# KV on four 64x64 tiles and two banks instead of two 128x64 tiles and one

## Chip, cores, metric

One core of one Trainium2 chip. The metric is the device time in microseconds (us) of one execution. The page and the trace of a kernel come from one profiled execution, whose span is 1.7 to 1.8 us shorter than its time (470.9 of 472.63 us before).

## The reference, cut to what matters

```python
qkv = (x @ wqkv)...                                   # x is 2048 x 1024, 32 heads of 32
kv  = jnp.einsum("bhsd,bhse->bhde", phi(k), v)        # branch A, linear attention
num = jnp.einsum("bhqd,bhde->bhqe", phi(q), kv)
a   = (num / den) @ wo
out = g * a + (1 - g) * b                             # b: a local attention over 8 positions
```

The kernel never forms v for branch A. It computes G = x^T phi(k) (1024 x 1024), then KV = Wv^T G for each pair of heads (a 64x64 block), and folds KV into the output weights ("W2").

## The kernel before

```python
# G: 16 banks, each 16 matmuls of 128x512, copied out by ScalarE            (cut)
for g in range(2):                                    # two groups of 16 heads
    kvp = ps_pj.tile([P, 512], F32, name="kv_ps", tag="pj")[:, 0:256].rearrange("p (c d) -> p c d", c=4)
    for c in range(4):
        for kt in range(KT):                          # KT = 8 blocks of 128 of the contraction
            for j in range(2):                        # two column tiles, 128 rows x 64 columns
                cols = slice(c * P + 64 * j, c * P + 64 * j + 64)
                nc.tensor.matmul(kvp[64 * j:64 * j + 64, c, :], lhsT=WvA[g][:, kt, cols],
                                 rhs=G[g][:, kt, cols], start=(kt == 0), stop=(kt == KT - 1))
    nc.vector.tensor_copy(out=KVT[:, 4 * g:4 * g + 4, :], in_=kvp)
WkB = load_w("WkB", B_wqkv, D, "wb")                  # into the buffers of WvA
...
w2_event(0, 0, ps_1, "p1", both)()                    # W2: 16 matmuls on 32x32 tiles; reads KVT of group 0
interleave(units, [(32, w2_event(0, 1, ps_1, "p1", both))])   # V projections, 128x512
```

The softmax here doesn't subtract the row's maximum and nothing guards it: scores larger than these inputs give would overflow.

## Time and profile before

| | before |
|---|---|
| time, median of the first 3 runs | 472.31 us (472.19 to 472.64) |
| profiled span, mean granted clock | 470.9 us, 1.000 |
| KV's first matmul to W2's first instruction | 116.38 to 118.53, 2.15 us |
| TensorE instructions in it | 256 (128 weight loads, 128 matmuls) |
| first V projection | 118.90 |

TensorE is the bound all along (busy for 99% of the span), so the table follows TensorE's time line. Most of the lines are in the prediction; the V projections that follow start so (start us, length us):

```profile
118.90 3.41 PE L294 MATMUL p_ps<-WvB,xT 128*128 128x512 bf16 x14
```

### The profile page before, as it was taken

To read this page: it belongs to the slowest core of one execution; us is meant where nothing else is said; L and a number is where in the kernel's file an instruction comes from. 1 tells how busy PE (TensorE), PEld (TensorE's weight loads), DVE (VectorE), ACT (ScalarE), POOL (GpSimd) and SP (SyncE) were. 2 spreads that over 40 slices of the span, in tenths; PEclk is the share of its full clock that TensorE was granted. 3 is DMA by queue.
4 is the path that set the end of the run, shared out by engine and by line. 5 is a ranking of instruction groups with operands and counts; after the bars stand their busy time and mean duration, and the time that the engine had idled before them with its cause. 6 is when DMAs were issued, how large, how long until landed. Compare 5 with 4: busy or idle time off the path is not lost.

```text
span 470.9 us, 13162 instructions
## 1 busy us (share of the span) xinstructions
PE 465.3 (99%) x5735; PEld 269.8 (57%) x5765; DVE 275.3 (58%) x598; ACT 169.1 (36%) x276; POOL 15.3 (3%) x30
## 2 busy tenths in 40 slices
PE   8999999999999999999999999999999999999997
PEld 5444444445444444444888888888874444444444
DVE  0596689990219999999666676767660049800000
ACT  1343321102433333334555555555553134221121
POOL 3300000500000000000000000000000000000000
PEclk9999999999999999999999999999999999999999
DMA  8999970000644233627325523442463923211001
GB/s 202 226 243 375 348 237 0 0 1 0 204 136 134 81 141 123 155 97 251 105 55 108 108 59 82 101 92 59 88 167 74 213 78 79 71 53 45 34 33 46
DMA packets 98732, 55.40 MB, mean 118 GB/s; under 512 B 70130, under 2 KB 90610, under 8 KB 98674
## 3 DMA queue, kind: packets, MB, share of 16 engines
q1 hardware_dynamic: 93378, 49.87, 39.9%
q10 hardware_dynamic: 5296, 4.69, 2.9%
q8 instruction: 45, 0.74, 0.6%
q14 instruction: 13, 0.11, 0.1%
HBM read 26.10 MB, written 15.86 MB: 89 GB/s over the span
## 4 chain that ended last, share of the span: by engine, by line
PE 86%; SPq 10%; DMA 2%; issue 1%; DVE 0%; DVEq 0%
PE q_ps L390 26%; PE d_ps L596 12%; PE p_ps L294 12%; PE e_ps L596 11%; PE g_ps L233 11%; PE p_ps L330 9%; SPq L115 4%; SPq L81 3%; DMA WvB<-in_B_wqkv_dram 2%; PE po L470 2%; PE s2b L448 2%; SPq L94 1%; SPq L98 1%; SPq L89 1%; SPq L119 1%
## 5 line engine op out<-in xcount | busy, mean ns | idle before, releaser
L390 PE MATMUL q_ps<-xT,WqB 64*64 64x512 bf16 x1024 | 70.3, 377 | 0.0
L390 PE MATMUL q_ps<-xT,WkB 64*64 64x512 bf16 x1024 | 69.8, 376 | 0.0
L156 DVE TENSOR_SCALAR e<-e 128x512 f32<-128x512 f32 x64 | 27.0, 423 | 68.3 <-ACT e L155 68.3
L294 PE MATMUL p_ps<-WvB,xT 128*128 128x512 bf16 x250 | 56.9, 379 | 0.3
L182 PE MATMUL pk_ps<-WkA,xT 128*128 128x512 bf16 x251 | 55.6, 381 | 0.7 <-DMA xT<-in_A_x_dram 0.4
L233 PE MATMUL g_ps<-pk,xrow 128*128 128x512 bf16 x251 | 55.2, 379 | 0.3
L453 ACT ACTIVATE PT<-s2b 128x928 bf16<-128x928 f32 (+4 forms) x40 | 34.2, 856 | 50.0 <-PE s2b L448 49.0
L455 DVE TENSOR_TENSOR PT<-PT,mask 128x928 bf16<-128x928 bf16 (+4 forms) x40 | 23.6, 590 | 36.3 <-ACT PT L453 36.3
L390 PEld LDWEIGHTS <-WkB 64*64 64x64 bf16 x1024 | 40.4, 107 | 6.9 <-DMA vd<-tmp 0.2
L330 PE MATMUL p_ps<-WqA,xT 128*128 128x512 bf16 x188 | 43.2, 379 | 0.3
L596 PEld LDWEIGHTS <-pqT 128*128 128x128 bf16 x272 | 26.0, 98 | 29.6 <-issue 0.2
L596 PEld LDWEIGHTS <-OBT 128*128 128x128 bf16 x272 | 26.0, 98 | 29.4
L182 PEld LDWEIGHTS <-xT 128*128 128x128 bf16 x256 | 25.1, 98 | 31.0 <-DMA xT<-in_A_x_dram 0.7
L390 PEld LDWEIGHTS <-WqB 64*64 64x64 bf16 x1024 | 39.4, 107 | 5.6 <-DVE qz L430 0.2
L233 PEld LDWEIGHTS <-xrow 128*128 128x128 bf16 x256 | 25.0, 98 | 30.2
L294 PEld LDWEIGHTS <-xT 128*128 128x128 bf16 x256 | 24.9, 98 | 30.2 <-issue 0.5
L603 DVE TENSOR_SCALAR osb<-e_ps,omg 128x128 bf16<-128x128 f32 x1 | 0.4, 351 | 57.6 <-PE e_ps L596 57.6
L155 ACT ACTIVATE e<-pk_ps 128x512 f32<-128x512 f32 x32 | 18.9, 597 | 40.6 <-PE pk_ps L182 36.4
L470 PEld LDWEIGHTS <-PT 64*56 64x56 bf16 (+2 forms) x1152 | 29.9, 104 | 4.5
L299 ACT CAST tmp<-p_ps 128x512 bf16<-128x512 f32 x32 | 18.7, 589 | 37.0 <-PE p_ps L294 26.6
L330 PEld LDWEIGHTS <-xT 128*128 128x128 bf16 x192 | 18.8, 98 | 22.6
L596 PE MATMUL d_ps<-WoA,pqT 128*128 128x512 bf16 (+1 forms) x133 | 30.7, 369 | 0.2
(63 smaller groups left out, 540.8 us busy)
## 6 DMA issues: line engine op xcount, KB each, us to landing
vd<-tmp SPq DMA_DIRECT2D x16, 264.0 KB
xrow<-in_A_x_dram SPq DMA_DIRECT2D x4, 1024.0 KB
out_dram<-osb ACTq DMA_DIRECT2D x31, 128.0 KB
pqd<-tmp SPq DMA_DIRECT2D x12, 256.0 KB
WvA<-in_A_wqkv_dram SPq DMA_DIRECT2D x2, 1024.0 KB
WoA<-in_A_wo_dram SPq DMA_DIRECT2D x2, 1024.0 KB
WvB<-in_B_wqkv_dram SPq DMA_DIRECT2D x2, 1024.0 KB
WqA<-in_A_wqkv_dram SPq DMA_DIRECT2D x2, 1024.0 KB
```

The source lines that it names most:

```text
L115: nc.sync.dma_start_transpose(out=xT[:, :, t * P:(t + 1) * P], in_=rows(x, t * P, (t + 1) * P))
L155: nc.scalar.activation(out=e[:], in_=pj[:], func=ACT.Exp)
L156: nc.vector.tensor_scalar(out=e[:], in0=e[:], scalar1=1.0, scalar2=1e-6, op0=ALU.min, op1=ALU.add)
L182: nc.tensor.matmul(pj[:], lhsT=xT[:, kt, t * P:(t + 1) * P], rhs=WkA[half][:, kt, :], start=(kt == 0), stop=(kt == KT - 1))
L233: nc.tensor.matmul(pj[:], lhsT=xrow[:, t, kt * P:(kt + 1) * P], rhs=pk[:, t, half * 512:(half + 1) * 512], start=(t == 0), stop=(t == NB - 1))
L294: nc.tensor.matmul(st["pj"][:], lhsT=xT[:, kt, t * P:(t + 1) * P], rhs=WvB[half][:, kt, :], start=(kt == 0), stop=(kt == KT - 1))
L330: nc.tensor.matmul(st["pj"][:], lhsT=xT[:, kt, t * P:(t + 1) * P], rhs=WqA[half][:, kt, :], start=(kt == 0), stop=(kt == KT - 1))
L390: nc.tensor.matmul(banks[o][64 * j:64 * j + 64, :], lhsT=lhsT(r, kt, j), rhs=rhs(r, kt), start=first and kt == 0, stop=kt == KT - 1, skip_ ...
L453: nc.scalar.activation(out=pt[:, :, 0:W_], in_=s2b[:].rearrange("p a b s -> p (a b) s")[:, :, 0:W_], func=ACT.Exp, scale=SCALE)
L455: nc.vector.tensor_tensor(out=pt[:, :, 0:W_], in0=pt[:, :, 0:W_], in1=mask[:, None, base:base + W_].broadcast_to([P, 4, W_]), op=ALU.mult)
L470: nc.tensor.matmul(o2[64 * h:64 * h + w, par, s_, i, :], lhsT=pt[r, i, o:o + w], rhs=V[r, m, 4 * c + i, :], start=True, stop=True)
L596: nc.tensor.matmul(st["ps"][:, 0:n], lhsT=lhsT, rhs=W[c0 // 512][:, c, c0 % 512:c0 % 512 + n], start=(side == 0 and c == 0), stop=(side == ...
```

## The change

The contraction of 128 rows is cut into two halves of 64, each on its own row tile (a block of the array's rows); with the two column halves that makes four 64x64 tiles working side by side. The two row halves are put in a bank each (a bank is one block of the memory that matmuls write; that two row tiles need two banks was the author's premise), so VectorE copies one bank out and adds the other. The intent: fill the array with four small products at once.

```diff
-                kvp = ps_pj.tile([P, 512], F32, name="kv_ps", tag="pj")[:, 0:256].rearrange("p (c d) -> p c d", c=4)
+                kvp = [ps_pj.tile([P, 512], F32, name="kv_ps", tag="pj")[:, 0:256].rearrange("p (c d) -> p c d", c=4)
+                       for _ in range(2)]
                 for c in range(4):
                     for kt in range(KT):
-                        for j in range(2):
+                        for r, j in ((0, 0), (1, 1), (0, 1), (1, 0)):
+                            rs = slice(64 * r, 64 * r + 64)
                             cols = slice(c * P + 64 * j, c * P + 64 * j + 64)
-                            nc.tensor.matmul(kvp[64 * j:64 * j + 64, c, :], lhsT=WvA[g][:, kt, cols],
-                                             rhs=G[g][:, kt, cols], start=(kt == 0), stop=(kt == KT - 1))
-                nc.vector.tensor_copy(out=KVT[:, 4 * g:4 * g + 4, :], in_=kvp)
+                            nc.tensor.matmul(kvp[r][64 * j:64 * j + 64, c, :], lhsT=WvA[g][rs, kt, cols],
+                                             rhs=G[g][rs, kt, cols], start=(kt == 0), stop=(kt == KT - 1))
+                kvf = junk.tile([P, 4, 64], F32, name="kvf", tag="kvf")
+                nc.vector.tensor_copy(out=kvf[:], in_=kvp[0])
+                nc.vector.tensor_tensor(out=KVT[:, 4 * g:4 * g + 4, :], in0=kvf[:], in1=kvp[1], op=ALU.add)
```

## The prediction

> **What bounds the kernel now.** I read the page's head and its chain of waits, then the stretch in which KV is computed, then the stages that already run four 64x64 tiles at once.
>
> ```profile
> PE 465.3 (99%) x5735; PEld 269.8 (57%) x5765; DVE 275.3 (58%) x598; ACT 169.1 (36%) x276; POOL 15.3 (3%) x30
> PEclk9999999999999999999999999999999999999999
> ...
> PE 86%; SPq 10%; DMA 2%; issue 1%; DVE 0%; DVEq 0%
> ...
> q8 instruction: 45, 0.74, 0.6%
> ```
>
> TensorE is busy for 99% of the span at full clock, and the chain that ends last runs on it (86%; the rest is the loading before 63 us). Whatever TensorE loses or gains after 63 us moves the end by as much. So the change is worth what it does to TensorE between the end of G and the first V projection. The timeline of 114 to 122 us has that stretch (columns: start us, length us, engine, line):
>
> ```profile
> 116.38 2.10 PEld L253 LDWEIGHTS <-WvA 128*64 128x64 bf16 x128 [0.42 <-issue]
> 116.38 2.22 PE L253 MATMUL kv_ps<-G,WvA 128*64 128x64 bf16 x128
> ...
> 117.63 0.42 DVE L255 CAST KVT<-kv_ps 128x256 bf16<-128x256 f32 x1 [10.53 <-PE kv_ps L253]
> 118.53 0.14 PEld L165 LDWEIGHTS <-KVT 32*32 32x32 bf16 x16
> 118.53 0.43 PE L165 MATMUL w_ps<-WoA,KVT 32*32 32x512 bf16 x16
> 118.64 0.42 DVE L255 CAST KVT<-kv_ps 128x256 bf16<-128x256 f32 x1 [0.59 <-PE kv_ps L253]
> ```
>
> The whole of KV is 128 matmuls, 2.15 us from 116.38 to the next product's start at 118.53. That is 0.46% of 472.31 us: were it free, the kernel would still be "within 2%". Deleting it would give 470.2 us; doubling it, 474.5. What is left to predict is the pace of the new stream and two waits behind it.
>
> The pace: a matmul here lasts 0.20 us (its latency), so the last of the 128 starts 2.22 - 0.20 = 2.02 us after the first, 15.9 ns apart. In the trace they start in couples (column halves j = 0 and 1, 3 to 4 ns apart), one couple every 31.6 ns: 64 rounds of two tiles, 64 x 31.6 = 2.02 us. The question is whether a round of four tiles takes as long as a round of two. The PV product already shows that form (start order of its tiles the same as the change's):
>
> ```profile
> 349.39 0.41 PE L470 MATMUL po<-V,PT 64*57 64x33 bf16 x32
> ```
>
> Latency is 0.18 us, so 32 starts span 0.23 us: 7.4 to 7.6 ns each, 30 ns for a round of four, with 57 weight columns and only 33 columns streamed. In another PV batch, 56-column tiles repeat every 28.5 ns and 64-column tiles every 32 ns. The round follows the weight columns [...], not the 33 streamed ones and not the number of tiles.
>
> [...] 128x64 (KV) and 64x64 (PV) both repeat about every 32 ns. So halving the rows shortens nothing. [...] In the trace, the matmul after each switch starts [...] (309 ns after a 512-column one into KV, 125 ns from KV into the 32x32 product). The change has the same number of switches, so nothing here. [...]
>
> **The change, part by part.**
> Removed: 128 pairs on two 128x64 tiles, 64 rounds x 31.6 ns = 2.02 us.
> Added: 256 pairs on four 64x64 tiles. There are still 2 groups x 4 chunks x 8 contraction blocks = 64 rounds, each with 64 weight and 64 streamed columns. 64 x 31.6 to 32 ns = 2.02 to 2.05 us. Gain: none; +0.00 to +0.03 us. The array has half its rows per matmul and twice the matmuls, the same work per round.
> VectorE: each group keeps a cast and gets an add. PSUM with f32 from SBUF costs no more than a cast: in the groups, line 157 (two inputs) takes 692 ns at 512 columns, like line 169's VectorE cast (686), and line 255's cast 425 at 256 columns; so an add is about 425 ns, and 40 ns lies between dependent instructions (ratio and omg lines). VectorE was idle 10.53 us before, so its 2 x 0.47 us cost nothing as work. As a wait: group 0 ends near 117.4 as before, cast 117.64 to 118.07, add 118.11 to 118.53, and some 50 ns until TensorE sees it: 118.58 to 118.60. The W2 product started at 118.53. Estimated loss 0.05 to 0.07 us. Group 1's add is read only by W2 at 215 us; it pushes VectorE's two W2 copies from 119.05 to about 119.55, and their banks are not wanted until the second W2 near 125.6 us. Nothing.
> Banks: four of the four rotating ones are used, not two. Group 1's second bank was G's last; ScalarE's copy of it ends at 116.49 + 0.59 = 117.08, before 117.4. The V projections, next in rotation, find bank 0 free at 118.07, banks 1 and 3 at 118.53 and about 119.5; they reach bank 3 after 3 x 8 matmuls of 0.216 us, at 124. Nothing.
> Sum of the sure terms: about +0.1 us, 472.4 us.
>
> **The rivals.**
> First, the instruction supply. KV now asks 4 TensorE instructions per round, 127 per us in all; after the change 8, about 253 per us for 2 us, 512 instructions. The trace of before shows nothing so dense: its best run of 64 takes 0.24 us, but its best run of 256 is KV's own, 1.95 us. In the trace the q8 packets start when 146 + 256k recorded TensorE instructions are done (659 at 69.21 us, 914 at 96.89). The next crossing lay 0.57 us into KV, near 116.95; its packet started at 117.83 and landed at 118.78, 1.83 us after the crossing, and 215 of the next 256 instructions had been used. After the change the crossing comes about 72 instructions into KV, 0.28 us, 116.67; landing at 118.50. If only one block is in hand, TensorE runs out 256 instructions later, at 117.68, and stands for about 0.8 us (0.5 to 0.9, as [...]packets took 0.9 to 1.4 us). The 0.07 us of the add then disappears behind it. Result about 473.1. For it: the margin of 41 was never exceeded in the trace. [...]
> Second, the sequencer can't issue 4 ns per instruction for long. For it: runs over 96 instructions never go below 7.1 ns in the trace. Against: those are spaced by the array's own rounds. At 6 ns, 512 would take 3.07 us, +1.05; at 7.5 ns, +1.8. Result 473.4 to 474.2.
> Third, a true gain: if the round were bound by 128 rows filling, 64x64 rounds would be shorter. The 28.5 ns rounds at 56 columns would allow 0.2 us at best (472.1); the 32 ns at 64 columns speaks against it.
>
> **Range and chances.** I give the sure terms alone 40%, the supply stall 40%, slow issue 15%, a gain 5%. Weighted: 0.40 x 0.1 + 0.40 x 0.8 + 0.15 x 1.4 - 0.05 x 0.2 = +0.56, put at 472.8 us. The range is 471.9 (no loss, and a run 0.4 lower than before's median) to 473.9 (slow issue at about 7 ns). 2% is 9.4 us, more than four times the whole KV stage: 98% within, 1% either side.
>
> **What would show it.** In the profile after: 256 KV matmuls; if their starts span 2.0 us, with couples of couples every 32 ns, the pace was right; a single hole of 0.5 to 0.9 us in them, ending as a q8 packet lands, is the supply stall; an even spacing of 5 to 8 ns is slow issue. In the first case the W2 product should start at 118.58 to 118.63. VectorE should show two adds near 0.42 us. Wrong would be: a round clearly under 30 ns, an add far from 0.42 us, or any shift of more than 0.3 us after 119 us that did not begin in KV.

What is cut from the prediction, where marked, no trace of this case shows; no term of its sum is among it. The sure terms came to about +0.1 us, 472.4 us; weighted with the rivals, the sum was +0.56, put at 472.8. These measured numbers stand:

- Blocks: the 45 packets of the instruction queue have 16 KiB each (0.74 MB). Those at 69.21 and 96.89 us start 255 recorded TensorE instructions apart, the same two in the trace of after 256 apart (the trace of before has 5735 matmuls for 5765 loads, so some records are missing). How many blocks are in hand isn't shown.
- The stall's range of 0.5 to 0.9 us rested in part on a cut term; run-out (117.68) and landing (118.50) give 0.8.
- The switches are changes of tile form. A matmul after a 512-column one of its own form starts 215 to 216 ns later in the trace of before, the first KV matmul 309 ns later: 0.09 us for a switch.
- The 50 ns from VectorE's end to TensorE: 51 and 52 ns in the trace of before (a qz written at 225.19 and at 327.80 us, the load that waited for it at 225.24 and 327.85).

## The result, and the profile after

Median 476.25 us (474.97 to 477.00, 6 runs) against 472.34 us (6 runs): ratio 1.0079, interval 1.0064 to 1.0094. Slower by 3.9 us, still within 2%, and outside the predicted range. (A ratio is the mean time of one kernel's runs over that of the other's runs of the same rounds, so not quite the ratio of the medians.) The six runs fall in two kinds: mean clock 0.996 in four (476.12 to 477.00) and 1.000 in two (474.97 and 475.54).

The page of the kernel after: head, clock by slice, instruction queue, chain.

```profile
PE 469.0 (99%) x5893; PEld 262.6 (55%) x5893; DVE 276.1 (58%) x600; ACT 169.1 (36%) x276; POOL 15.4 (3%) x30
...
PEclk9999999999899999999999999999999999999999
...
q8 instruction: 46, 0.75, 0.7%
...
PE 98%; DMA 1%; issue 0%; DVE 0%; DVEq 0%
```

TensorE is as much the bound as before, one slice shows a lower clock, and there is one block of instructions more. Lines of the timeline of 114 to 126 us of the kernel after (start us, length us, engine, line, what; in brackets the engine's idle time before it and what ended it):

```profile
116.05 1.68 PEld L255 LDWEIGHTS <-WvA 64*64 64x64 bf16 x187 [0.42 <-issue]
116.05 1.78 PE L255 MATMUL kv_ps<-G,WvA 64*64 64x64 bf16 x186
...
117.35 0.42 DVE L258 COPY kvf<-kv_ps 128x256 f32<-128x256 f32 x1 [10.59 <-PE kv_ps L255]
...
117.88 0.42 DVE L259 TENSOR_TENSOR KVT<-kvf,kv_ps 128x256 bf16<-128x256 f32 x1
119.87 0.76 PE L255 MATMUL kv_ps<-G,WvA 64*64 64x64 bf16 x70 [2.04 <-issue]
119.87 0.64 PEld L255 LDWEIGHTS <-WvA 64*64 64x64 bf16 x69 [2.15 <-issue]
120.55 0.14 PEld L165 LDWEIGHTS <-KVT 32*32 32x32 bf16 x16
120.55 0.43 PE L165 MATMUL w_ps<-WoA,KVT 32*32 32x512 bf16 x16
...
120.92 5.31 PE L298 MATMUL p_ps<-WvB,xT 128*128 128x512 bf16 x16
```

In the middle of group 1, after 186 of 256 matmuls, TensorE stands: from 117.63 (last start) to 119.87, 2.24 us. "issue" means that it waited for no semaphore and no engine. The loads stop at 187 and the matmuls at 186: the weights for the next matmul are loaded and the matmul itself is missing. Windows of the same trace (granted clock is the number after TensorE's, VectorE's and the others' busy times):

```profile
117.65:118.50 0.85, 0.18 (x22) 0.07 (x9) 0.55 (x2) 0.00 (x0) 0.00 (x0) 1.00 0.06 10
118.50:119.85 1.35, 0.00 (x0) 0.00 (x0) 0.00 (x0) 0.00 (x0) 0.00 (x0) 1.00 0.89 287
119.85:121.40 1.55, 1.53 (x89) 1.02 (x89) 0.61 (x2) 0.29 (x1) 0.00 (x0) 1.00 1.10 375
121.40:124.80 3.40, 3.40 (x10) 1.19 (x9) 1.43 (x3) 1.37 (x3) 0.00 (x0) 0.50 0.94 309
```

From 121.4 to 124.8, 3.41 us long, the clock is half, and the V matmuls start 425 ns apart where they start 215 ns apart in the trace of before.

Where the 4.3 us between the two profiled spans (470.9 and 475.2) lie, by the starts of TensorE's stages:

| stretch | before | after | difference |
|---|---|---|---|
| start to KV's first matmul | 116.38 | 116.05 | -0.33 (run to run) |
| KV's first matmul to W2 | 2.15 | 4.50 | +2.35: the stop 2.24, the pace 0.13 |
| first V to first Q of branch A | 17.74 | 19.44 | +1.70: the half clock |
| first scores to the first output product | 131.53 | 132.14 | +0.61 (see below) |

Two causes carry it: a stop that waits for nothing the profile shows, and a half-clock window behind it.

### The profile page after: what moved, and what is told of

Its sections match the earlier page's. It is cut to its first block, busy times and chain, and to the rows that moved or that the text cites. A ratio compares the mean times of both kernels' runs of the same rounds, so it can differ in the third digit from the quotient of the medians.

```text
span 475.2 us, 13453 instructions
## 1 busy us (share of the span) xinstructions
PE 469.0 (99%) x5893; PEld 262.6 (55%) x5893; DVE 276.1 (58%) x600; ACT 169.1 (36%) x276; POOL 15.4 (3%) x30
## 4 chain that ended last, share of the span: by engine, by line
PE 98%; DMA 1%; issue 0%; DVE 0%; DVEq 0%
PE q_ps L394 26%; PE p_ps L298 12%; PE d_ps L600 12%; PE pk_ps L182 12%; PE g_ps L233 12%; PE e_ps L600 11%; PE p_ps L334 9%; PE po L474 2%; PE s2b L452 2%; DMA xT<-in_A_x_dram 1%; PE kv_ps L255 1%; PE w_ps L165 0%; DVE osb L607 0%; DVEq L607 0%
## 5 line engine op out<-in xcount | busy, mean ns | idle before, releaser
L298 PE MATMUL p_ps<-WvB,xT 128*128 128x512 bf16 x256 | 59.1, 387 | 0.0
L394 PEld LDWEIGHTS <-WkB 64*64 64x64 bf16 x1024 | 37.8, 107 | 8.6 <-DMA vd<-tmp 0.2
L394 PEld LDWEIGHTS <-WqB 64*64 64x64 bf16 x1024 | 36.7, 107 | 8.0 <-issue 0.6
L474 PEld LDWEIGHTS <-PT 64*56 64x56 bf16 (+2 forms) x1152 | 27.7, 104 | 6.9 <-issue 0.2
```

What stands on the lines that cost most here:

```text
L298: nc.tensor.matmul(st["pj"][:], lhsT=xT[:, kt, t * P:(t + 1) * P], rhs=WvB[half][:, kt, :], start=(kt == 0), stop=(kt == KT - 1))
L394: nc.tensor.matmul(banks[o][64 * j:64 * j + 64, :], lhsT=lhsT(r, kt, j), rhs=rhs(r, kt), start=first and kt == 0, stop=kt == KT - 1, skip_ ...
L474: nc.tensor.matmul(o2[64 * h:64 * h + w, par, s_, i, :], lhsT=pt[r, i, o:o + w], rhs=V[r, m, 4 * c + i, :], start=True, stop=True)
```

## The experiments

**Theory.** TensorE runs out of fetched instructions. In the trace of after, a 16 KiB packet (16384 bytes, as are all 46) of the instruction queue starts at 117.55 and lands at 118.49, while TensorE stands; TensorE goes on 1.38 us after the landing. **Rivals.** The tile form itself (row tiles in two banks, or VectorE reading one bank while TensorE writes another); the add; the 2 MB of WkB, whose first packet moved at 118.42, delaying the block; something tied to a place in KV.

| kernel | pairs in KV | stop after matmul | length us | packet landed, TensorE went on | median us (runs) | ratio to before [interval] |
|---|---|---|---|---|---|---|
| after | 256 | 186 | 2.24 | 118.49, 119.87 | 476.25 (6) | 1.0079 [1.0064, 1.0094] |
| e1_cols32 | 256 | 186 | 2.31 | 119.27, 120.65 | 476.10 (4) | 1.0075 [1.0057, 1.0092] |
| e3_late_wkb | 256 | 186 | 2.66 | 119.13, 120.48 | 476.72 (4) | 1.0082 [1.0065, 1.0100] |
| e7_no_add | 256 | 186 | 2.69 | 119.07, 120.44 | 476.79 (4) | 1.0095 [1.0072, 1.0118] |
| e4_shift20 | 256 | 166 | 2.31 | 118.42, 119.69 | 475.81 (4) | 1.0069 [1.0054, 1.0084] |
| e5_shift51 | 256 | none; in W2 | 2.29 | 119.78, 121.10 | 476.27 (4) | 1.0072 [1.0053, 1.0092] |
| e6_before_shift51 | 128 | none | | | 472.76 (4) | 1.0004 [0.9989, 1.0019] |
| e8_half | 192 | 186 | 1.71 | 118.46, 119.90 | 474.47 (4) | 1.0041 [1.0026, 1.0056] |
| e2_split | 256 | none | | | 473.38 (4) | 1.0018 [1.0003, 1.0033] |

**1. The same number of instructions without row tiles, second bank or add.**

```diff
-                        for j in range(2):
-                            cols = slice(c * P + 64 * j, c * P + 64 * j + 64)
-                            nc.tensor.matmul(kvp[64 * j:64 * j + 64, c, :], lhsT=WvA[g][:, kt, cols],
+                        for j in range(4):
+                            cols = slice(c * P + 64 * (j // 2), c * P + 64 * (j // 2) + 64)
+                            lc = slice(c * P + 32 * j, c * P + 32 * j + 32)
+                            nc.tensor.matmul(kvp[32 * j:32 * j + 32, c, :], lhsT=WvA[g][:, kt, lc],
```

> The kernel before with KV on four 128x32 tiles: also 256 pairs of weight load and matmul, but full 128-row contraction, one bank, no second bank and no add. Theory (TensorE runs out of fetched instructions): the recorded TensorE instruction stream again stops after instruction 1472 of the trace (KV starts near 1100, so after about matmul 186 of 256) for 2.0 to 2.4 us, KV takes 3.9 to 4.4 us, and the median is 474.5 to 477, with a half-clock window in some runs. Rival (two row tiles in two banks, or the add, cause the stop): no stop, KV 1.8 to 2.1 us, 472.0 to 472.6.

Timeline of e1_cols32:

```profile
116.81 1.73 PE L254 MATMUL kv_ps<-G,WvA 128*32 128x64 bf16 x186
...
120.65 0.73 PE L254 MATMUL kv_ps<-G,WvA 128*32 128x64 bf16 x70 [2.12 <-issue]
```

Again after 186 matmuls, again 2.3 us, and the same time. So neither row tiles nor two banks nor the add make the stop. VectorE reads a finished bank during group 1 here too, but it does so in the kernel before as well (117.63), which doesn't stop. (The trace numbers the last instruction 1462, not 1472, because ten matmul records of earlier stages are missing; counted by matmul it is the same place.)

**2. Is it the add, or the load of WkB?** In e7_no_add the group is copied from one bank (wrong result, relative error 0.05); in e3_late_wkb the loads of WkB wait for a small VectorE memset behind the second W2.

```diff
-                nc.vector.tensor_copy(out=kvf[:], in_=kvp[0])
-                nc.vector.tensor_tensor(out=KVT[:, 4 * g:4 * g + 4, :], in0=kvf[:], in1=kvp[1], op=ALU.add)
+                nc.vector.tensor_copy(out=KVT[:, 4 * g:4 * g + 4, :], in_=kvp[0])
+                nc.vector.tensor_copy(out=seen1[:, g:g + 1], in_=kvp[1][:, 0, 0:1])
```

> The changed kernel without VectorE's add: group copied from the first bank only (wrong result on purpose), the second bank touched by a copy of one column. Theory: the stop and the time stay, 474.5 to 477. Rival (the wait for the add, or VectorE reading one bank while TensorE writes others, holds TensorE): no stop, about 472.4.

```diff
-            WkB = load_w("WkB", B_wqkv, D, "wb")
...
+            for h in range(2):                        # behind the interleave of the V units and the second W2
+                wk = wpool.tile([P, KT, 512], BF16, name=f"WkB{h}", tag="wb")
+                nc.vector.memset(wk[:, 0, 0:1], 0.0)
+                nc.sync.dma_start(out=wk[:], in_=B_wqkv[:, D + h * 512:D + h * 512 + 512]
...
```

> The changed kernel with the load of WkB held back until VectorE has done its W2 copies, so that its 2 MB don't move while the instruction block is fetched. Theory (a fixed time from asking to having a block): the stop stays at 2.0 to 2.4 us, 474.5 to 477. Rival (the WkB packets, which start within 0.1 us of the block's landing, delay the block's use): the stop shrinks to about 0.8 us, ending near the landing of the instruction packet, no half-clock window, 472.9 to 473.5.

Windows of e3_late_wkb (the last two numbers are the share of the DMA engines and GB/s):

```profile
117.80:119.10 1.30, 0.22 (x26) 0.11 (x14) 0.59 (x2) 0.00 (x0) 0.00 (x0) 1.00 0.05 13
119.10:120.50 1.40, 0.02 (x4) 0.01 (x4) 0.00 (x0) 0.00 (x0) 0.00 (x0) 1.00 0.00 0
120.50:122.00 1.50, 1.50 (x87) 1.00 (x87) 0.52 (x2) 0.00 (x0) 0.00 (x0) 0.65 0.00 0
```

Nothing moves but the instruction packet, which lands at 119.13, and TensorE still stands until 120.48. Both stops are longer than in the kernel after (2.66 us here, where 2.0 to 2.4 was expected, and 2.69 in e7_no_add): the packet started 1.95 us after KV's first matmul, in the kernel after 1.50 us. Add and WkB are out as causes.

**3. Does the stop belong to KV or to the instruction stream?** More and narrower warm-up matmuls at the very start put 40 or 102 TensorE instructions more ahead of KV.

```diff
-                    nc.tensor.matmul(warm[:], lhsT=ones, rhs=ones, start=True, stop=True)
+                    nc.tensor.matmul(warm[:, 0:83], lhsT=ones, rhs=ones[:, 0:83], start=True, stop=True)
-            warm_up(37)
+            warm_up(57)
```

> The changed kernel with 57 warm-up matmuls of 83 columns in place of 37 of 128 (40 more TensorE instructions in about the same time at the start). Theory (the stop comes at a block boundary of the instruction stream): the stop moves 20 matmuls earlier in KV, after about matmul 166 of 256 in place of 186, still at recorded instruction 1472; its length stays 2.0 to 2.4 us, the time 474.5 to 477. Rival (the stop belongs to a place in KV or to a moment in time): it stays at matmul 186.

Timeline of e4_shift20:

```profile
115.96 1.61 PE L255 MATMUL kv_ps<-G,WvA 64*64 64x64 bf16 x166
...
119.69 1.33 PE L255 MATMUL kv_ps<-G,WvA 64*64 64x64 bf16 x90 [2.12 <-issue]
```

Twenty pairs more in front, and the stop comes twenty matmuls earlier. e5_shift51 has `warm_up(88)` with 54 columns.

> The changed kernel with 88 warm-up matmuls of 54 columns (102 more TensorE instructions than the changed kernel). Theory: KV starts at recorded instruction about 1202, the block from 1472 has been fetched by then, so KV runs through in 2.1 us, and the stop comes at the next boundary, 1728, which lies after 512 KV instructions and about 14 of the 32 instructions of the first W2 product; 2.0 to 2.6 us; the time stays 474.5 to 477. Rival: the stop stays at matmul 186 of KV.

Timeline of e5_shift51:

```profile
116.48 2.36 PE L255 MATMUL kv_ps<-G,WvA 64*64 64x64 bf16 x256
...
118.78 0.11 PEld L165 LDWEIGHTS <-KVT 32*32 32x32 bf16 x8
118.78 0.41 PE L165 MATMUL w_ps<-WoA,KVT 32*32 32x512 bf16 x7
...
121.10 0.41 PE L165 MATMUL w_ps<-WoA,KVT 32*32 32x512 bf16 x9 [1.91 <-issue]
```

KV runs through in one piece, and the stop falls in the middle of W2, after 15 of its 32 instructions (14 were expected). Counted from the program's start in the traces, the stop comes after 736 weight loads in the kernel after and in e4_shift20, and after 864 here: 128 pairs, or 256 instructions, further. So the stop belongs to a border between blocks of 256, the step at which the packets start too (recorded instructions 665 and 921 at 68.94 and 96.58 us in the trace of after). The stage is no faster for it: the shift moves the stop and doesn't take it away.

> The kernel before with the same 88 narrower warm-up matmuls: what the shift itself costs. Theory: KV has 128 pairs, no stop anywhere in it; 472.0 to 472.8 (0 to 0.5 us for the longer start). Rival: none; a control.

The control: the same shift in the kernel before costs 0.0004 of the time, within its interval of nothing, and KV has no stop.

**4. Half the change.** Group 0 on 64x64 tiles, group 1 as before (the loop of before under `if g == 1`).

> Group 0 on 64x64 tiles in two banks with the add, group 1 as in the kernel before: 192 pairs. Theory: the stream stops again after recorded instruction 1472, now 58 of 64 matmuls into group 1, about 1.9 us after KV's start, and until the block is there, some 3.7 us after it: 1.6 to 2.0 us, so nearly the whole loss for half the change; 473.8 to 476.5. Rival (a cost per matmul on 64x64 tiles): half the loss, about 473.4 without a half-clock window.

Timeline of e8_half:

```profile
116.11 1.24 PE L264 MATMUL kv_ps<-G,WvA 64*64 64x64 bf16 x128
...
117.28 1.11 PE L255 MATMUL kv_ps<-G,WvA 128*64 128x64 bf16 x58
...
119.90 0.28 PE L255 MATMUL kv_ps<-G,WvA 128*64 128x64 bf16 x6 [1.51 <-issue]
```

128 + 58 is once more 186 pairs, now in the old form, six matmuls before the end. The block comes 3.8 us after KV's start as in the kernel after; less time was left to wait. All four runs kept the full clock.

**5. Thinning the instructions out.** The changed kernel, with 16 V matmuls (long ones, few instructions: 32 in 3.5 us) between the groups; e12_before_split is the same split of the kernel before.

```diff
-            for g in range(2):
+            def kv_group(g):
...
+            kv_group(0)
-            w2_event(0, 0, ps_1, "p1", both)()
-            interleave(units, [(32, w2_event(0, 1, ps_1, "p1", both))])
+            interleave(units, [(16, second), (16, w2_event(0, 0, ps_1, "p1", both)),   # second: kv_group(1), loads WkB
+                               (32, w2_event(0, 1, ps_1, "p1", both))])
```

> The changed kernel with 16 V matmuls (32 instructions, 3.5 us) between the two KV groups; the same 256 pairs, banks and adds. Theory (instruction supply): no gap over 0.3 us in either KV group, each group about 1.05 us, full clock, two more mode switches of 0.1 us each: 472.4 to 472.9. Rival (the tile form or the add stops the array): the stop stays in group 1, 474.5 to 477.

> The split version of the changed kernel once more, to be compared with the next: 0.3 us of KV and mode switches over the kernel before, and what else is lost in the later stage: 472.7 to 473.5, clock 1.0 throughout, no gap in KV.

> The kernel before (128x64 tiles, 128 pairs) with the same split: group 1 and the first W2 product behind 16 V matmuls. It tells what the split itself costs. Theory: two more mode switches, 0.2 us: 472.4 to 472.9, and the split changed kernel within 0.3 us of it. Rival (64x64 tiles cost something of their own besides the stop): the split changed kernel over 0.5 us slower than this one.

Timelines of e11_split_again (the kernel of e2_split in another job):

```profile
116.24 1.24 PE L255 MATMUL kv_ps<-G,WvA 64*64 64x64 bf16 x128
...
120.97 1.24 PE L255 MATMUL kv_ps<-G,WvA 64*64 64x64 bf16 x128
```

and of e12_before_split:

```profile
115.99 1.20 PE L253 MATMUL kv_ps<-G,WvA 128*64 128x64 bf16 x64
...
120.68 1.20 PE L253 MATMUL kv_ps<-G,WvA 128*64 128x64 bf16 x64
```

No stop, full clock in all runs: with 3.5 us of thin instructions between, the same 256 pairs, banks and adds cost about 3 us less. The first job gave 473.38 us, above the expected 472.4 to 472.9; its trace has one stop of 0.62 us at 304 us, in the dense 64x64 stage, so part of it was lost there (24 x 256 instructions behind the border in KV, so at a block border again). The second gave 472.80 (473.05, 474.83, 472.71, 472.87, 472.53, 472.73), ratio 1.0013 [0.9999, 1.0027]; the split of before 472.57, ratio 1.0009 [0.9994, 1.0023]. The tile form in itself so costs about 0.2 us by the medians, which the intervals can't tell from nothing; the trace shows 0.04 us in each group (1.24 against 1.20).

**6. Is the half clock a second cost of any stop?** The kernel before, with VectorE copies put ahead of the one that W2 waits for: TensorE waits on a semaphore, and not for instructions: the packet of this stretch landed at 118.86, over 2 us before the wait ended.

```diff
+                if g == 0:
+                    kvf = junk.tile([P, 4, 64], F32, name="kvf", tag="kvf")
+                    for _ in range(7):                # e10_wait4: 4
+                        nc.vector.tensor_copy(out=kvf[:], in_=kvp)
                 nc.vector.tensor_copy(out=KVT[:, 4 * g:4 * g + 4, :], in_=kvp)
```

> The kernel before with seven extra VectorE copies of group 0's bank ahead of its real one, so that TensorE stands for a known time between KV and the first W2 product with plenty of fetched instructions: 7 x 0.41 us more on the wait, less 0.44 us of slack, W2 at about 121.0 in place of 118.53, a gap of 2.6 us. Theory (a stop of over 2 us alone brings the half clock): some or most runs at a mean clock of 0.996 with one window of 3.4 us at half clock, 476.0 to 476.7; the others at clock 1.0, 474.6 to 475.3. Rival (the half clock comes from the dense 64x64 stream): clock 1.0 in every run, all at 474.6 to 475.3.

> The same with four extra copies: a gap of about 1.35 us, W2 at about 119.75. Theory: too short for the half clock; clock 1.0 in every run, 473.4 to 474.1. Rival: half-clock windows here too, 475 and more.

Timeline and windows of e9_wait7:

```profile
121.07 0.44 PE L165 MATMUL w_ps<-WoA,KVT 32*32 32x512 bf16 x16 [2.59 <-DVE KVT L259]
```

```profile
122.00:123.00 1.00, 1.00 (x4) 0.30 (x2) 0.88 (x2) 0.70 (x2) 0.00 (x0) 0.50 0.81 256
123.00:124.00 1.00, 1.00 (x4) 0.35 (x3) 0.00 (x0) 0.00 (x0) 0.00 (x0) 0.50 1.01 360
```

A gap of 2.79 us between starts, made by a semaphore, brings the same half-clock window of 3.41 us (from 121.94) and the same cost behind the stop: first V to first Q takes 19.44 us, to the hundredth what it takes in the kernel after. So the half clock is a cost of the stop and needs neither 64x64 tiles nor missing instructions. In time: median 477.20 us, ratio 1.0100 [1.0087, 1.0113]; e10_wait4 473.82 us, 1.0037 [1.0022, 1.0051]. The gap of 1.41 us in e10_wait4 gave clock 1.000 in all four runs; three lie at 473.63 to 474.00 as expected, and the profiled one at 475.72 began KV 1.8 us late (118.18): its first 128x512 matmuls start 427 ns apart until 9.5 us and 216 ns apart from then on, with 10 of them from 6.0 to 9.5 us where e9_wait7 has 18. Half missed in e9_wait7: the two runs with clock 1.000 took 477.16 and 477.47 us, where 474.6 to 475.3 were expected. They have no trace. A late start like that of e10_wait4 would account for it; it isn't shown.

Why only some runs are hit can be read from the traces. In each of the six traces with a half clock behind the stop, it begins 116.05 us after the first clock record in the trace file, which is 34 stretches of 3.41 us. So a grid of 3.41 us, laid from that first record, gives in every trace the stretch in which TensorE stood. In the kernel after, in e1_cols32 (full clock in its profiled run, with a stop of 2.31 us) and in e8_half it reads (the number after the stretch's length is TensorE's busy time):

```profile
117.97:121.39 3.42, 1.52 (x89) 1.01 (x89) 0.94 (x3) 0.28 (x1) 0.00 (x0) 1.00 0.86 284
```

```profile
116.07:119.48 3.41, 2.47 (x190) 1.82 (x189) 0.42 (x1) 0.59 (x1) 0.39 (x2) 1.00 0.08 20
119.48:122.90 3.42, 2.20 (x91) 1.36 (x92) 1.44 (x3) 1.03 (x2) 0.00 (x0) 1.00 0.98 310
```

```profile
118.38:121.79 3.41, 1.85 (x30) 0.92 (x29) 1.57 (x3) 1.07 (x2) 0.00 (x0) 1.00 1.01 321
```

After the stretches with TensorE busy for 1.52 us or less (0.87 in e9_wait7, 0.92 in e7_no_add, 0.94 in e3_late_wkb, 1.30 in e4_shift20, 1.45 in e5_shift51, 1.52 in the kernel after) the clock is half in all six; after 1.85 (e8_half), 2.20 (e10_wait4) and 2.20 (e1_cols32, where a border of the grid cuts the stop into 1.14 and 1.17 us) it stays full. In these nine traces, then, it is how much of one stretch the stop takes that decides, and not its length alone; nothing between 1.52 and 1.85 us was measured.

## Why the prediction was wrong

- **The pace of four tiles: right.** A round of four was to take 31.6 to 32 ns. It took 31.6 at first and 33.3 later; KV without its stop took 2.15 us in place of 2.02. The reading behind it, that the round follows the weight columns and not the streamed ones, held less well: with half the weight columns (e1_cols32, 64 streamed) the first rounds of four still took 29 ns.
- **Add, banks, W2's wait: right, and without effect.** The add took 422 ns (425 predicted), began 0.10 us after the copy (0.04 predicted) and ended at 118.30, while TensorE stood anyway. Without it nothing changed (e7_no_add).
- **The stop itself: right in kind, as the first rival, at 40%; its times partly by luck.** TensorE was to run out about 117.68 and did at 117.63; the packet was to land at 118.50 and did at 118.49. But this run began KV 0.33 us early. Counted from KV's start, the run-out came after 1.58 us, not 1.30, because the fetched instructions reached 44 further than assumed, and the landing after 2.44 us, not 2.12. (The place of the crossing is a little off too: by the prediction's own count it lies about 80 recorded instructions into KV, not 72.)
- **The step that failed: "landing at 118.50 ... stands for about 0.8 us".** It took the landing of the packet for the moment at which the instructions can run. In seven traces TensorE went on 1.27 to 1.44 us after the landing. The term was 2.24 us, not 0.8: 0.86 us up to the landing, as predicted, and 1.38 us behind it that the prediction didn't have.
- **A term that was left out: the half clock.** A stop of over 2 us in a stage that never stopped was not followed to what the clock does. It cost 1.70 us in the profiled run, and four of six runs had it. The traces show a half-clock window of 3.41 us (3413 ns in the trace of after), a grid of that step that starts elsewhere in every run (the first clock record lies 6.245 us into the span before, 5.333 us after), and the busy times of experiment 6.
- **Slow issue: true only in a trace of it.** The pairs settled to 8.3 ns, about 4.2 ns an instruction, where 5 to 8 were to show it; worth 0.13 us. With 128x32 tiles (e1_cols32) they settled to the same gaps of 8, 8 and 9 ns. What sets them isn't shown.
- **The range was too narrow for its own rival**: 0.8 us for a stop whose end was not measured in the trace of before, since there it never came to one.

Not settled: how many blocks are held in all (only that the stream stops at a border between blocks of 256 when the next block isn't there yet fits every run), what fills the 1.3 to 1.4 us after the landing, and the +0.61 us in the later stage of the one profiled run. In the latter there is a gap of 0.28 us exactly 20 x 256 instructions after the big stop (5118 matmuls and loads and 2 semaphore instructions), so at a block border too. e1_cols32, e3_late_wkb and e8_half lost nothing there, while e6_before_shift51 and e9_wait7, with KV as before, lost 0.21 us.

## What to carry to other kernels

Splitting a product into smaller tiles multiplies instructions, and the instruction stream is a resource like any other: count how many an engine takes in the time that the next block of 256 needs (in the six traces with the stop in KV, TensorE went on 3.7 to 4.3 us after the dense stretch began), and put long instructions between dense stretches. In the kernel after, a dense stretch of 512 TensorE instructions, about 4 ns each, stopped the engine after 373; before, 256 in 1.95 us didn't. No version here beats the kernel before; a round of four small tiles took as long as one of two (31.6 to 33.3 ns against 31.6), so there was nothing to gain. And when TensorE stops, look at the clock behind the stop: here it cost up to 1.70 us more, and whether it did hung on where the stop fell in the clock's window.
